# Moving the preparation of the first MLP's output weights eight attention slots later

## The chip, the cores and the metric

The kernel runs on one NeuronCore of a Trainium2 chip, as one program launch. The metric is the device time of that launch in microseconds, the median of several runs. The engines are named as the profile names them: PE is TensorE's matmul side and PEld its weight loads, DVE is VectorE, ACT is ScalarE, POOL is GpSimd and SP is SyncE, whose queue issues the DMAs here.

## The reference: attention with a learned bias, then two MLPs

- Attention over 4 batches, 8 heads, 576 positions, head size 64: `softmax(q k^T / 8 + bias) v`. The bias of head h at row i and column j is a small two-layer net (hidden size 32, ReLU) of `log1p(|i-j|) / log1p(max(i,1))`; it is the same for all batches.
- The result becomes 2304 tokens of 512 numbers.
- First MLP: `h = max(x w1, x w2, x w3)` with 768 columns, then `h w_out`, 768 x 512. These `w_out` weights (`moe_w_out`, `mwo` in the kernel) are the ones the change is about.
- Second MLP: 2048 columns, a quadratic gate, and an output product back to 512.

MLP weights arrive as 64-bit numbers and are turned on the chip into a sum of two float16 parts, hi and lo; products use three matmuls (hi hi, hi lo, lo hi).

## The kernel before: slots, queues and a planner

**Slots.** Attention is cut into 144 slots. A unit is one block j of 128 query rows and one batch b; each of its 8 heads is a slot. Blocks 0, 1 and 2 take slots 0 to 31, 32 to 63 and 64 to 95, 8 per batch; the last 48 slots alternate the short block (64 rows, called SJ, 4 slots per batch) and block 3. In a slot `emit_s` (L691) makes the scores of the next slot on PE, `emit_soft` adds the bias and takes the row's extreme on DVE (L705), takes the exponential on ACT (L707), makes hi and lo (L723 on ACT, L724 and L725 on POOL) and has them transposed by DMA (L727). Three slots later `emit_pv` (L747) multiplies by v.

**Bias.** The bias table of block j+1 is built during block j by 18 `bias_group` calls: a mask on DVE (L389), 16 matmuls (L393), and an eviction on DVE (L399, L400) or on ACT and POOL (L402 to L405) in turn. They need a table of logarithms that a DMA brings (`xtable`, L297, or L302 for the short block) and that is scaled on DVE (L307). Block 2's groups are written for slots 44 to 59.

**First MLP.** When a pair of batches of a block is done, its items go into a queue: 18 `mlp1` groups of 12 matmuls (L802, evicted by L807 on ACT or L809 on DVE, hi and lo by L813 and L814), then 4 `mlp2` groups of 18 matmuls (L824) which need the output weights. Each slot takes items at a fixed rate (2 a slot in block 0, then 1.2, 1.5, ...). Until the output weights are ready, `next_mlp` hands out `mlp1` items of block 0 alone.

**Output weights.** `conv_wo` has 12 pieces and an end. Pieces 1 to 6 each load 128 rows (L450), decode them (L462, L463, L465 on ACT, L464 on DVE), and sum magnitudes on PE for a scale (L481, L483). The decoded numbers stay in a scratch tile, `zt` and `rt_`, parts of `ws`. Pieces 7 to 12 split one stripe each into hi and lo (L157 on ACT, L158 on DVE) in the tile `wo`. Then `wo_done` is set. The parameter `woz` is the first slot that takes decode pieces (0.7 a slot, `c0`), `wo` the first that takes split pieces (1 a slot, `c1`) and from which, once all is done, `next_mlp` hands out everything:

```python
if i >= (WO if n_wo[0] >= NF1 else PRM["woz"]):
    with sooner("wo"):
        for _ in range(rate("conv", PRM["c0"] if n_wo[0] < NF1 else PRM["c1"])):
            if n_wo[0] != NF1 or i >= WO:
                n_wo[0] += 1
                next(pieces, None)
with sooner("mlp"):
    for _ in range(rate("mlp", PRM["mlp"][u.j])):
        e = next_mlp(i >= WO and (wo_done or not PRM["ww"]))
```

The raw buffers for these loads serve the first MLP's input weights until slot 13, and later the second MLP's weights. `rt_` is taken by the short block's `xtable` (L302), which is written for slot 64; its scaling for slot 85.

**Order.** The program text gives priorities (bias groups rank 400 instructions sooner); a planner that simulates the engines lists each engine's instructions, taking what is ready, also from far ahead in the text. The engines then work through their lists in order.

Of the kernel before, what the change touches and what calls it, by code (L numbers as in the profile page):

```python
# [20 lines left out]
def kernel(ctx: ExitStack, tc: tile.TileContext, qt, kt, vr, small, mw1, mw2, mw3, mwo, win, wo2, out):  # L21
# [17 lines left out]
        pin=0,  # L39
        ww=1,  # L40
        vb='pppp',
        woz=28,
        c1=1,
        ef=1,
        vl=[0, 0, 2, 11],
        vm=[0, 0, 8, 15],
        vs=[0, 0, 11, 19],
        wo=38,
        cm=[0, 3, 6, 9, 13, 16],
        veng='vv',  # L50
        weng='vvv',
# [41 lines left out]
    def st(shape, dt, tag):  # L93
        return sb.tile(shape, dt, tag=tag, name=tag, bufs=BUFS.get(tag, 1))
# [3 lines left out]
    wo = st([P, NF1, 512], U32, "wo")  # L98
# [1165 lines left out]
```

## Time and profile before

| what | us |
|---|---|
| median of 3 runs | 1012.7 |
| lowest and highest run | 1000.15, 1017.84 |
| profiled execution, its own time | 1012.1 |
| span of its instructions | 1010.3 |
| PE busy in the span | 927.0 |
| DVE busy | 700.4 |
| ACT busy | 600.4 |
| POOL busy | 511.7 |

Times in a trace are counted from the first instruction, so they add up to the span; the device time of the same execution is 1.8 us more. A view by stretches gives, for each stretch of the span, how long each engine was busy. A timeline gives for each instruction, or a run of equal ones, its start, its length, and in brackets how long its engine had been idle before it and what ended that.

### The profile page before, as it was taken

What the parts mean: (1) busy time and instruction counts of PE and PEld (TensorE: products, weight loads), DVE (VectorE), ACT (ScalarE), POOL (GpSimd) and SP (SyncE); (2) the same over time, 40 slices, a digit from 0 to 9 for tenths busy, and PEclk for the clock granted to TensorE, in tenths of its full rate; (3) what the DMA queues carried; (4) which work ended last, traced back from release to release, by engine and by line L of the source; (5) the groups of instructions that cost most, each with busy time, mean ns of one, the idle gap of its engine ahead of it and who ended that gap; (6) DMA issues with size and microseconds to landing.
All of it is one profiled execution on the core that took longest, in us unless ns stands there. A gap on an engine that the chain in (4) does not pass through costs nothing. (4 is left out here: it accounts for less than half of the span.)

```text
span 1010.3 us, 25953 instructions
## 1 busy us (share of the span) xinstructions
PE 927.0 (92%) x10258; PEld 757.4 (75%) x10258; DVE 700.4 (69%) x1551; ACT 600.4 (59%) x1194; POOL 511.7 (51%) x734
## 2 busy tenths in 40 slices
PE   5758889889999999999999888998999999999996
PEld 5636668678888878778777777543588888888885
DVE  8987877767756686556455487886686587586565
ACT  4788865855656545868577689543354444444342
POOL 4132577666777765646457011997134343344442
PEclk8777979999999999999999999999999999999999
DMA  9896989998998979999999654010020010000000
GB/s 301 247 290 140 245 190 229 207 237 170 207 259 186 187 180 209 215 223 235 209 188 197 184 196 137 22 35 8 1 85 22 1 43 23 1 22 13 10 22 22
DMA packets 238970, 141.47 MB, mean 140 GB/s; under 512 B 187520, under 2 KB 217728, under 8 KB 238336
## 3 DMA queue, kind: packets, MB, share of 16 engines
q1 hardware_dynamic: 238688, 139.55, 58.6%
q8 instruction: 80, 1.31, 0.5%
q14 instruction: 42, 0.34, 0.1%
q10 hardware_dynamic: 160, 0.26, 0.1%
HBM read 79.68 MB, written 15.27 MB: 94 GB/s over the span
## 5 line engine op out<-in xcount | busy, mean ns | idle before, releaser
L802 PEld LDWEIGHTS <-aw 128*128 128x128 f16 x2160 | 190.3, 99 | 46.2 <-issue 24.6
L802 PE MATMUL pm<-xT,aw 128*128 128x256 f16 (+1 forms) x1812 | 202.3, 264 | 7.4 <-ACT hl L829 2.6
L725 POOL TENSOR_TENSOR phl<-sp,phl 128x512 f16<-128x512 f32 x136 | 161.3, 1186 | 0.0
L707 ACT ACTIVATE sp<-sp,mx 128x576 f32<-128x576 f32 x144 | 110.4, 767 | 68.0 <-DVE mx L705 67.7
L691 PE MATMUL s<-k,qz 64*128 64x288 f32 (+1 forms) x576 | 126.2, 449 | 15.4 <-DVE mx L705 13.0
L724 POOL TENSOR_TENSOR phl<-sp,phl 128x64 f16<-128x64 f32 x136 | 49.8, 366 | 178.7 <-ACT phl L723 153.2
L705 DVE CUSTOM_DVE_ANT_0 sp<-s,ab 128x576 f32<-128x576 f32 x128 | 93.3, 752 | 28.4 <-POOL phl L725 10.4
L1142 ACT ACTIVATE sp<-pm,vec 128x256 f32<-128x256 f32 x112 | 61.4, 556 | 81.3 <-PE pm L1125 78.2
L691 PEld LDWEIGHTS s<-k,qz 64*128 64x128 f32 (+1 forms) x576 | 69.1, 195 | 34.6 <-DVE mx L705 15.3
L723 ACT ACTIVATE phl<-sp 128x576 f16<-128x576 f32 x136 | 89.8, 672 | 4.7 <-DMA pt<-phl 3.8
L747 PEld LDWEIGHTS <-pt 128*128 128x128 f16 x1792 | 73.0, 100 | 25.2 <-DMA pt<-phl 16.2
L1146 POOL TENSOR_TENSOR hh<-hh 128x128 f32<-128x128 f32 x56 | 32.9, 588 | 106.4 <-DVE hh L1144 90.3
L747 PE MATMUL pav<-v,pt 128*128 128x64 f16 x1568 | 70.5, 196 | 12.3 <-DMA pt<-phl 11.9
L1125 PEld LDWEIGHTS <-ab 128*128 128x128 f16 x756 | 73.8, 98 | 9.2
L1143 DVE SCALAR_TENSOR_TENSOR hh<-pm,vec,sp 128x256 f32<-128x256 f32 x112 | 52.5, 478 | 33.5 <-ACT sp L1142 33.2
L824 PE MATMUL pm<-hh,wo 128*128 128x256 f16 x558 | 71.3, 279 | 2.6 <-POOL hh L814 1.0
L824 PEld LDWEIGHTS <-wo 128*128 128x128 f16 x648 | 62.2, 100 | 14.7 <-issue 6.5
L814 POOL TENSOR_TENSOR hh<-hm,hh 128x256 f16<-128x256 f32 (+1 forms) x60 | 44.8, 746 | 51.9 <-ACT hh L813 51.7
L1164 PEld LDWEIGHTS <-xT 128*128 128x128 f16 x588 | 57.4, 98 | 7.8 <-ACT xT L1151 1.2
L1164 PEld LDWEIGHTS <-wo 128*128 128x128 f16 x588 | 57.5, 98 | 6.7
L809 DVE SCALAR_TENSOR_TENSOR hm<-pm,hm 128x256 f32<-128x256 f32 (+1 forms) x108 | 42.0, 389 | 28.6 <-PE pm L802 12.3
L1147 POOL TENSOR_TENSOR hh<-hh 128x128 f32<-128x128 f32 x56 | 26.2, 468 | 68.6 <-DVE hh L1144 66.3
(300 smaller groups left out, 1999.0 us busy)
## 6 DMA issues: line engine op xcount, KB each, us to landing
k<-in_k_dram SPq DMA_DIRECT2D x64, 288.0 KB, 3.8
v<-v_d SPq DMA_DIRECT2D x24, 640.0 KB, 4.9
ws<-in_moe_w_out_dram SPq DMA_DIRECT2D x15, 512.0 KB, 4.9
ws<-in_moe_w_in_dram SPq DMA_DIRECT2D x9, 512.0 KB, 6.0
x_d<-hl SPq DMA_DIRECT2D x36, 128.0 KB, 2.5
qz<-in_q_dram SPq DMA_DIRECT2D x16, 256.0 KB, 4.5
ab<-in_moe_w_dram SPq DMA_DIRECT2D x8, 512.0 KB, 9.8
qz<-x_d SPq DMA_DIRECT2D x4, 1024.0 KB, 4.8
```

Source lines behind the costliest of these rows:

```text
L691: last_score[0] = T.matmul(sbox[i + r][:, c, :288], q[p, s if u.j == SJ else s // 2], k[p, 288 * c:288 * c + 288], start=True, stop=True)
L705: last_pair[0] = V.tensor_tensor_reduce(halves(sn), sbox.pop(i)[:, :, :288], halves(bias_sb[u.j][:, h]), -0.125, 3e38, ALU.add, ALU.min, mx)
L707: last_soft[0] = A.activation(pf, sn, AF.Exp, scale=-1.0, bias=mx, accum_out=u.sums[:, h:h + 1])
L723: A.activation(hl[:, :S], pf, AF.Copy)
L725: G.tensor_tensor(hl[:, S + 64:], pf[:, :512], hl[:, :512], ALU.subtract)
L747: T.matmul(u.pav[:, 64 * h:64 * h + 64], pt[:, c], v[:, sl, 64 * (h % 4):64 * (h % 4) + 64], **kw)
L802: T.matmul(o, wm[:, ft, i, wp, kk], x_rhs(key, xp, kk) if n == 256 else x_rhs(key, xp, kk)[:, c], start=(x == 0), stop=(x == 11))
L824: T.matmul(pm, wo16[:, ft, wp, P * d:P * d + P], hh[:, ft, hp], start=(ft == 0 and y == 0), stop=(ft == NF1 - 1 and y == 2))
L1125: T.matmul(pm, w[:, wp, kk], x2t[ORDER[y]][:, kk, xp, 256 * sub:256 * sub + 256], start=(x == 0), stop=(x == 11))
L1142: A.activation(r, pm, AF.Relu, scale=c_ch[:, f], bias=c_half)
L1143: V.scalar_tensor_tensor(t, pm, c_c[:, f], r, ALU.mult, ALU.max)
L1164: T.matmul(m[x], gl[:, gp, i], w[:, wp], start=(start and z == 0 and x % 2 == 0), stop=(stop and z == 2 and (x % 2 == 1 or x == 6)))
```

## The change

Two of the planner's parameters: decode pieces of the first MLP's output weights begin at slot 36, not 28, and their splits, with the output products behind them, from slot 46 on, not 38.

```diff
         pin=0,
         ww=1,
         vb='pppp',
-        woz=28,
+        woz=36,
         c1=1,
         ef=1,
         vl=[0, 0, 2, 11],
         vm=[0, 0, 8, 15],
         vs=[0, 0, 11, 19],
-        wo=38,
+        wo=46,
         cm=[0, 3, 6, 9, 13, 16],
```

## Rows read from the trace of the kernel before

**Rows 1.** The page's head: span, and busy time and instructions by engine.

```profile
span 1010.3 us, 25953 instructions
...
PE 927.0 (92%) x10258; PEld 757.4 (75%) x10258; DVE 700.4 (69%) x1551; ACT 600.4 (59%) x1194; POOL 511.7 (51%) x734
```

**Rows 2.** Busy time by stretches: length, engines' busy time (instructions), clock, DMA, GB/s.

```profile
core 0: us, PE busy (x) PEld busy (x) DVE busy (x) ACT busy (x) POOL busy (x), PEclk, DMA share, GB/s
...
125.00:150.00 25.00, 20.69 (x270) 16.49 (x269) 17.37 (x37) 17.07 (x37) 19.49 (x27) 0.73 0.87 186
150.00:175.00 25.00, 22.55 (x486) 21.02 (x483) 20.80 (x43) 11.14 (x31) 20.06 (x24) 1.00 0.98 246
175.00:200.00 25.00, 20.79 (x245) 15.82 (x243) 19.35 (x65) 21.74 (x49) 15.82 (x23) 1.00 0.96 200
200.00:225.00 25.00, 20.73 (x279) 18.25 (x278) 15.21 (x39) 15.81 (x35) 14.85 (x20) 0.99 1.12 243
225.00:250.00 25.00, 25.00 (x364) 21.01 (x363) 16.06 (x35) 13.16 (x33) 14.42 (x20) 0.94 0.79 163
250.00:275.00 25.00, 24.86 (x357) 21.02 (x355) 18.07 (x39) 16.30 (x41) 20.78 (x25) 1.00 1.06 218
```

**Rows 3.** Timeline of DVE: scores of slots 31, 32, 45, 46, 48.

```profile
147.09 0.76 DVE L705 CUSTOM_DVE_ANT_0 sp<-s,ab 128x576 f32<-128x576 f32 x1
...
174.27 0.76 DVE L705 CUSTOM_DVE_ANT_0 sp<-s,ab 128x576 f32<-128x576 f32 x1 [0.82 <-POOL ab L405]
...
199.21 0.76 DVE L705 CUSTOM_DVE_ANT_0 sp<-s,ab 128x576 f32<-128x576 f32 x1
...
211.07 0.75 DVE L705 CUSTOM_DVE_ANT_0 sp<-s,ab 128x576 f32<-128x576 f32 x1
...
230.27 0.75 DVE L705 CUSTOM_DVE_ANT_0 sp<-s,ab 128x576 f32<-128x576 f32 x1
```

**Rows 4.** Groups by line, 147.8 to 174.2 us: busy us, mean ns, idle before.

```profile
L462 ACT ACTIVATE ws<-ws 128x512 f32<-128x512 f32 x3 | 2.1, 685 | 2.2 <-DMA ws<-in_moe_w_out_dram 2.2
...
L464 DVE SCALAR_TENSOR_TENSOR ws<-ws 128x512 uint32<-128x512 uint32 x1 | 1.1, 1056 | 0.0
```

**Rows 5.** Timeline of ACT: the first decode and the bias eviction behind it.

```profile
151.54 0.68 ACT L462 ACTIVATE ws<-ws 128x512 f32<-128x512 f32 x1 [1.52 <-DMA ws<-in_moe_w_out_dram]
...
154.97 0.37 ACT L402 ACTIVATE btmp<-pm 128x256 f32<-128x256 f32 x1
```

**Rows 6.** Timelines of POOL and DVE: two decodes and a POOL subtraction.

```profile
184.74 1.16 POOL L725 TENSOR_TENSOR phl<-sp,phl 128x512 f16<-128x512 f32 x1
...
184.97 1.47 DVE L464 SCALAR_TENSOR_TENSOR ws<-ws 128x512 uint32<-128x512 uint32 x1 [0.77 <-ACT ws L463]
...
188.28 0.69 DVE L464 SCALAR_TENSOR_TENSOR ws<-ws 128x512 uint32<-128x512 uint32 x1 [0.88 <-ACT ws L463]
```

**Rows 7.** Timelines of ACT, DVE and PE: the six splits and PE's wait.

```profile
204.21 3.78 ACT L157 ACTIVATE wo<-ws,vec 128x512 f16<-128x512 f32 x6
...
204.96 4.81 DVE L158 SCALAR_TENSOR_TENSOR wo<-ws,vec,wo 128x512 f16<-128x512 f32 x6 [1.27 <-ACT wo L157]
...
209.19 1.47 PE L802 MATMUL pm<-xT,aw 128*128 128x256 f16 x12 [0.79 <-ACT hm L807]
```

**Rows 8.** Timelines of DVE and PE: two table scalings, matmuls around the second.

```profile
177.16 0.52 DVE L307 TENSOR_SCALAR xtab<-xtab,vec 128x576 f32<-128x576 f32 x1 [1.25 <-DMA xtab<-log_d]
...
221.89 0.37 DVE L307 TENSOR_SCALAR ws<-ws,vec 128x288 f32<-128x288 f32 x1 [5.68 <-DMA ws<-log_d]
...
217.99 2.13 PE L824 MATMUL pm<-hh,wo 128*128 128x256 f16 x18
...
222.92 0.64 PE L393 MATMUL pm<-coef,masks 128*128 128x64 f16 x16 [2.75 <-DVE masks L389]
...
224.24 3.63 PE L824 MATMUL pm<-hh,wo 128*128 128x256 f16 x18 [0.62 <-DVE ab L400]
```

**Rows 9.** Timelines of POOL and DVE: block 2's last bias group, slot 64.

```profile
271.88 1.05 POOL L405 TENSOR_TENSOR ab<-ab,btmp 128x256 f32<-128x256 f32 x1
...
284.07 0.76 DVE L705 CUSTOM_DVE_ANT_0 sp<-s,ab 128x576 f32<-128x576 f32 x1 [1.26 <-PE s L691]
```

## The prediction, made before the change was run

> **What bounds the kernel now.** I read the page first: TensorE is busy 927.0 of 1010.3 us [rows 1]. The busy time by stretches of 25 us says where the rest could be won. From 225 us on, PE is busy for 25.00 and 24.86 us of 25 [rows 2]; before that it idles 4.31, 2.45, 4.21 and 4.27 us in the four stretches from 125 to 225 us, 15.24 us together. The slots that the change names lie just there. The score instructions of VectorE (L705, one a slot in slot order) date the slots: slot 31 at 147.1 us, slot 32 at 174.3, slot 45 at 199.2, slot 46 at 211.1, slot 48 at 230.3 [rows 3]. So attention stands still for 27.2 us between blocks 0 and 1, while the bias table of block 1 is finished (the row of slot 32 names L405, the end of a bias group, as its releaser), then runs 14 slots in 25 us, then stops again around the splits of the first output weights. In 175 to 200 us ScalarE is the fullest engine, 21.74 of 25 us [rows 2].
>
> **What moves, by the code.** Decode pieces come at 0.7 a slot, splits at one a slot. Working the rates through, the six decodes are written at slots 29, 30, 32, 33, 35, 36 before and 37, 38, 40, 41, 43, 44 after; the six splits at 38 to 43 before and 46 to 51 after; the first output product (L824) is allowed at slot 44 before and 52 after. The 18 groups of mlp1 for token pair (0,1) may run either way (order below 2): at 1.2 a slot from slot 37 they are used up at slot 51, so no MLP turn is lost. From slot 55 on both versions write the same instructions in the same order. Nothing is added or removed; the change can only move PE's idle time between 147 us and about 260 us, and through the planner what follows. PE is full behind it, so I price each step by the PE idle it makes or removes. A gain through this window alone is at most the 15.24 us above.
>
> **Part by part**, against the profiled execution's own 1012.1 us (0.6 us under the median of the runs, 1012.7):
>
> 1. Decode 0 leaves the standstill of 147 to 174 us. There stand three L462 (685 ns each) and one L464 of 1056 ns [rows 4]. L464 sits on VectorE, which builds the bias: 1.1 us. ScalarE also waits for the raw weights before 151.54 us, and the next L402 (a bias group's eviction) follows only at 154.97 us [rows 5], but VectorE has other groups meanwhile. Ends: 0, and -2.45, all of PE's idle time in 150 to 175 us [rows 2]. I take -1.1, VectorE's row being the nearest.
>
> 2. The same work arrives at slots 37 to 41, where ScalarE is fullest: three L462 and the two other ScalarE instructions of decode 0, allowed the same length, 5 x 0.685 = 3.4 us. ScalarE's idle time there is 25 - 21.74 = 3.3 us [rows 2], scattered between waits. Ends 0 and +3.4; in between no row decides, and I take half, +1.7. VectorE's share is hidden by its 5.65 idle us there.
>
> 3. The six splits leave 204 to 210 us: 3.78 us of ScalarE and 4.81 us of VectorE in one block [rows 7]. PE lost 0.79 us to it, waiting for an eviction (L807) behind the block. Ends -0.8 and 0; I take -0.8.
>
> 4. They arrive at slots 46 to 51, one a slot, beside bias groups of block 2. Cover: VectorE is busy 15.21 and 16.06 us of 25 in the stretches from 200 to 250 us, and PE has mlp1 of (0,1) to fill with. Taken 0; without that cover +4.8, the VectorE block at its length.
>
> 5. The table load of the short block (L302) reuses the decode's scratch, so it waits for the last split; its scaling (L307) then stops VectorE until it lands: 5.68 us idle before 221.89 us. PE loses 2.75 us to it and comes back slow: 18 matmuls of L824 take 3.63 us where 18 took 2.13 just before [rows 8], and the granted clock of 225 to 250 us is 0.94 [rows 2], so 1.5 us more. After the change this falls later, beside a longer PE queue. Ends: -4.25 (another table's scaling waited 1.25 us only [rows 8]) and +2.9 (PE sees all 5.68). I take -1.5: the wait stays, the slow clock goes.
>
> 6. The DMAs move with it: six raw loads, two table loads, four result stores of the first output products and the first loads for the second MLP, all on SP's queue among the transposes. Their bytes are the same and the raw buffers are free long before, so 0; the raw loads' own waits on ScalarE (2.2 us of the standstill, [rows 4]) are in step 1's bounds.
>
> Sum: -1.1 + 1.7 - 0.8 + 0 - 1.5 = -1.7, so 1012.1 - 1.7 = 1010.4, **1010 us**. All low ends together: -2.45 - 0.8 - 4.25 = -7.5, 1005; all high ends: 3.4 + 4.8 + 2.9 = +11.1, 1023.
>
> **A port rule to weigh.** L464 takes 0.69 us at 188.28 us and 1.47 us at 184.97 us, where POOL is in a subtraction that began at 184.74 us and lasts 1.16 [rows 6]. A split has the same kind of operands, so at its new place, among POOL's bias and hi/lo work, I allow it 0.78 us more. The Trainium skill, SBUF — State Buffer, section "Who interferes with whom", says that VectorE and GpSimd share a read port that is locked for a whole instruction: a VectorE instruction with two SBUF inputs and a GpSimd one that reads SBUF exclude each other. The pair of rows agrees with it. By that rule all six splits are stretched, and the sum would be up to 6 x 0.78 = 4.7 us higher, an estimate of 1015 us, if nothing hides it; I keep it at 0 as in step 4, and its full length in rival A.
>
> **Rivals.**
>
> A, slower: VectorE cannot finish block 2's bias in time. It gets the splits stretched, 4.81 + 6 x 0.78 = 9.5 us, and the 5.68 us wait of step 5, 15.2 us, into the slots in which that bias is made. Its last group now ends at 271.88 + 1.05 = 272.9 us, and slot 64, which needs it, starts at 284.07 [rows 9]: 11.1 us of slack. Past that attention stands still as at 147 us; 15.2 - 11.1 = 4.1 us late, all idle on PE if nothing fills: 1016 us. For it: VectorE is the bias's engine and was late once already [rows 3]. Against: the first standstill cost PE only 2.45 us.
>
> B, faster by more: ScalarE free of the decode and its wait lets the L402 of 154.97 us go when the wait began, at 151.54 - 1.52 = 150.0 us, 5 us sooner; block 1 starts as much earlier, and the idle time of 150 to 175 us and of 200 to 225 us goes with the slow clock: 2.45 + 4.27 + 1.5 = 8.2, 1004 us. For it: ScalarE is busy 11.14 of 25 us there, mostly waiting. Against: VectorE is at 20.80 [rows 2].
>
> C, it does nothing: the planner takes whatever is ready. L302, written for slot 64, and L307, written for slot 85, run before slot 48 [rows 3, 8]; decodes whose data are in may be pulled back to the same idle places. 1012 us.
>
> D, the whole list is planned anew and a later stretch comes out otherwise. No row prices that; one more standstill like the 27 us one with PE unfed, or one less, is about 22 us either way: 990 or 1034.
>
> **How the numbers follow.** Forecast 0.46, A 0.14, B 0.14, C 0.12, D 0.07 on each side. The runs of the kernel before spread from 1000.15 to 1017.84 us, so the median to come can be some us off its trace; the range takes the bounds 1005 to 1023 and B, and a few us of spread beyond both: 997 to 1026. Two per cent (992 and 1033 us) is about what a measurement can tell from no change. Only D reaches it, and the tail of A: faster 0.07, same 0.85, slower 0.08.
>
> **What would show it.** Step 1: the gap between slots 31 and 32 shorter than 27.2 us by one or two. Step 2: ScalarE over 22 us busy in the 25 us after slot 32, with all six L464 there or later. Steps 3 and 4: splits one at a time, beside L389, and the first L824 after all of mlp1 (0,1). Step 5: L302 later than slot 48 and the wait of L307 without a fall of the granted clock. A: slot 64's score released by L405. C: L464 and the splits at the old times. The prediction is wrong if PE's idle time after 225 us changes by more than that before it.

## The result, and the profile after

| kernel | median, us | lowest to highest | runs |
|---|---|---|---|
| before | 1010.58 | 1000.15 to 1020.1 | 20 |
| after | 1017.36 | 1011.06 to 1023.17 | 20 |

The change makes the kernel slower: ratio 1.0074, 95% interval 1.0056 to 1.0093, so about 7.5 us with 1.9 us either way. Single executions of one kernel spread by up to about 1% to each side; the profiled one of after took 1016.85 us, its span 1015.1. Ratios, here and below, leave out single runs more than 1.5% above the fastest of their kernel, so they are not quite the quotient of the medians.

The page after, busy time of the engines (answers [rows 1]):

```profile
PE 922.4 (91%) x10258; PEld 754.4 (74%) x10258; DVE 702.7 (69%) x1551; ACT 599.8 (59%) x1194; POOL 515.1 (51%) x734
```

The instructions are the same in number on every engine. The first five stretches of [rows 2], with the same columns:

```profile
125.00:150.00 25.00, 21.77 (x288) 17.96 (x288) 16.95 (x37) 15.13 (x34) 18.88 (x27) 0.71 0.96 198
150.00:175.00 25.00, 19.33 (x401) 18.07 (x401) 18.12 (x36) 12.18 (x33) 17.21 (x21) 0.93 0.92 218
175.00:200.00 25.00, 23.22 (x322) 19.62 (x322) 16.18 (x49) 17.30 (x42) 15.43 (x23) 1.00 0.90 163
200.00:225.00 25.00, 18.63 (x270) 14.69 (x271) 18.34 (x56) 18.73 (x41) 16.83 (x21) 1.00 1.15 261
225.00:250.00 25.00, 23.53 (x311) 19.29 (x310) 20.18 (x39) 15.42 (x38) 19.49 (x24) 0.94 1.05 224
```

In 150 to 175 us PE idles 5.67 us (25 - 19.33) where it idled 2.45. Fixed stretches cut the work at another place in each kernel, so the rest is read by slots: the score instruction (L705) of a slot starts a stretch. Busy time by such stretches, kernel before, slots 31 to 32, 32 to 46, 46 to 64 and 120 to 143:

```profile
147.09:174.27 27.18, 24.73 (x552) 23.20 (x550) 22.38 (x44) 13.46 (x36) 22.62 (x28) 1.00 0.96 237
174.27:211.07 36.80, 31.80 (x370) 25.42 (x368) 28.19 (x85) 30.81 (x67) 22.83 (x33) 1.00 0.99 223
211.07:284.07 73.00, 69.38 (x985) 58.71 (x983) 46.02 (x105) 41.65 (x103) 50.45 (x65) 0.98 0.99 202
...
479.31:549.31 70.00, 65.44 (x834) 52.30 (x833) 34.30 (x89) 48.69 (x107) 39.66 (x56) 0.98 0.96 189
```

The same four of after:

```profile
144.94:176.70 31.76, 24.91 (x531) 23.43 (x528) 21.90 (x43) 14.93 (x38) 23.39 (x28) 0.95 0.92 204
176.70:215.70 39.00, 34.52 (x467) 28.16 (x464) 23.64 (x73) 28.77 (x66) 23.07 (x33) 1.00 1.02 210
215.70:285.30 69.60, 64.50 (x907) 54.38 (x908) 52.48 (x120) 44.27 (x107) 51.80 (x65) 0.98 0.96 208
...
480.39:552.93 72.54, 65.15 (x834) 52.30 (x833) 35.27 (x89) 48.68 (x107) 39.66 (x56) 0.98 0.94 183
```

From slot 31 to 64 TensorE does the same work but for two matmuls, 1907 before (552 + 370 + 985) and 1905 after, in 136.98 and 140.36 us. The standstill between slots 31 and 32 is 4.6 us longer, not shorter. From slot 64 on, each engine has the same instructions in the same order in both kernels; yet slots 120 to 143 take 2.5 us more in this trace.

What VectorE waited for in the standstill, kernel before (columns: what waited, for what; us in total, times, longest):

```profile
DVE btmp L399 <- PE pm L393: 2.0, 2, 1.7
DVE masks L389 <- PE pm L393: 1.4, 2, 0.8
DVE sp L705 <- POOL ab L405: 0.8, 1, 0.8
```

and after:

```profile
DVE ws L464 <- ACT ws L463: 2.7, 2, 1.4
DVE rd L756 <- ACT sp L707: 2.7, 1, 2.7
...
```

Two waits are new. One is for the decode (L463 to L464); one is for ScalarE's exponential (L707), at the first step of a finished unit's normalization (L756). The timelines of after show where both come from. ScalarE (start, us, instruction, idle before and its releaser): a wait for a hi/lo buffer with the exponential of slot 31 behind it, the raw-load waits and the block of splits:

```profile
147.74 0.68 ACT L723 ACTIVATE phl<-sp 128x576 f16<-128x576 f32 x1 [2.44 <-DMA pt<-phl]
148.33 0.76 ACT L707 ACTIVATE sp<-sp,mx 128x576 f32<-128x576 f32 x1
...
154.38 0.68 ACT L462 ACTIVATE ws<-ws 128x512 f32<-128x512 f32 x1 [1.42 <-DMA ws<-in_moe_w_out_dram]
...
157.50 0.66 ACT L462 ACTIVATE ws<-ws 128x512 f32<-128x512 f32 x1 [1.87 <-DMA ws<-in_moe_w_out_dram]
...
197.68 0.68 ACT L462 ACTIVATE ws<-ws 128x512 f32<-128x512 f32 x1 [2.12 <-DMA ws<-in_moe_w_out_dram]
...
205.99 0.68 ACT L463 ACTIVATE ws<-ws 128x512 uint32<-128x512 uint32 x1 [2.23 <-DMA ws<-in_moe_w_out_dram]
...
221.65 3.79 ACT L157 ACTIVATE wo<-ws,vec 128x512 f16<-128x512 f32 x6 [1.49 <-DVE vec L514]
```

VectorE of after: scores of slots 31 and 32 (as in [rows 3]; 45 is at 211.54, 46 at 215.70, 48 at 222.28), two decodes and one eviction of `mlp1` (L809) behind a late decode:

```profile
144.94 0.76 DVE L705 CUSTOM_DVE_ANT_0 sp<-s,ab 128x576 f32<-128x576 f32 x1
...
155.66 1.18 DVE L464 SCALAR_TENSOR_TENSOR ws<-ws 128x512 uint32<-128x512 uint32 x1 [1.33 <-ACT ws L463]
...
158.74 0.69 DVE L464 SCALAR_TENSOR_TENSOR ws<-ws 128x512 uint32<-128x512 uint32 x1 [1.37 <-ACT ws L463]
...
176.70 0.76 DVE L705 CUSTOM_DVE_ANT_0 sp<-s,ab 128x576 f32<-128x576 f32 x1
...
209.93 0.42 DVE L809 SCALAR_TENSOR_TENSOR hm<-pm,hm 128x256 f32<-128x256 f32 x1 [4.50 <-ACT hm L807]
```

TensorE of after, the matmuls that waited for those two engines, and the ones behind the splits:

```profile
157.09 0.63 PE L393 MATMUL pm<-coef,masks 128*128 128x64 f16 x16 [1.33 <-DVE hm L809]
159.44 1.00 PE L802 MATMUL pm<-xT,aw 128*128 128x128 f16 x12 [1.72 <-ACT hm L807]
...
209.95 0.93 PE L802 MATMUL pm<-xT,aw 128*128 128x256 f16 x7 [1.86 <-ACT hm L807]
...
223.39 0.49 PE L747 MATMUL pav<-v,pt 128*128 128x64 f16 x11 [3.50 <-DMA pt<-phl]
...
224.51 4.12 PE L802 MATMUL pm<-xT,aw 128*128 128x256 f16 x21
```

The first chain is to be read across the three: a raw row lands late, ScalarE waits 1.42 us at L462, VectorE waits 1.33 us at L464 for ScalarE's L463, with the eviction L809 queued behind it, and PE waits 1.33 us for L809. 3 us later it happens again: 1.87 us on ScalarE, 1.37 on VectorE, and PE waits 1.72 us for an eviction (L807) that ScalarE has queued behind the row. At 206 us it happens once more. The wait at L756 is not a raw row's, the first of which is asked for only at 148.6 us: ScalarE stands 2.44 us at L723, until 147.74 us, for a hi/lo buffer that a transposition still reads, and the exponential that L756 needs is queued behind. How long ScalarE waited for raw rows in all, kernel before (us, times):

```profile
  ACT ws L462: 3.7, 4
```

and after:

```profile
  ACT ws L462: 6.0, 4
  ACT ws L463: 2.2, 1
```

### The profile page after: what moved, and what is told of

It is laid out like the page before. It is cut to its first block, busy times and chain, and to the rows that moved or that the text cites. A ratio compares the mean times of both kernels' runs of the same rounds, so it can differ in the third digit from the quotient of the medians.

```text
span 1015.1 us, 25955 instructions
## 1 busy us (share of the span) xinstructions
PE 922.4 (91%) x10258; PEld 754.4 (74%) x10258; DVE 702.7 (69%) x1551; ACT 599.8 (59%) x1194; POOL 515.1 (51%) x734
## 5 line engine op out<-in xcount | busy, mean ns | idle before, releaser
L725 POOL TENSOR_TENSOR phl<-sp,phl 128x512 f16<-128x512 f32 x136 | 160.0, 1176 | 0.0
L707 ACT ACTIVATE sp<-sp,mx 128x576 f32<-128x576 f32 x144 | 110.6, 768 | 71.9 <-DVE mx L705 71.3
L691 PE MATMUL s<-k,qz 64*128 64x288 f32 (+1 forms) x576 | 121.3, 449 | 11.3 <-DVE mx L705 8.9
L705 DVE CUSTOM_DVE_ANT_0 sp<-s,ab 128x576 f32<-128x576 f32 x128 | 93.0, 751 | 31.0 <-PE s L691 13.4
L747 PEld LDWEIGHTS <-pt 128*128 128x128 f16 x1792 | 71.9, 100 | 30.1 <-DMA pt<-phl 21.4
L723 ACT ACTIVATE phl<-sp 128x576 f16<-128x576 f32 x136 | 89.9, 672 | 4.4 <-DMA pt<-phl 3.7
L1146 POOL TENSOR_TENSOR hh<-hh 128x128 f32<-128x128 f32 x56 | 35.6, 635 | 109.0 <-DVE hh L1144 94.3
L691 PEld LDWEIGHTS s<-k,qz 64*128 64x128 f32 (+1 forms) x576 | 66.5, 196 | 28.9 <-DVE mx L705 10.9
L1143 DVE SCALAR_TENSOR_TENSOR hh<-pm,vec,sp 128x256 f32<-128x256 f32 x112 | 52.5, 478 | 36.0 <-ACT sp L1142 35.9
L824 PE MATMUL pm<-hh,wo 128*128 128x256 f16 x558 | 68.5, 273 | 1.9 <-ACT hh L813 1.1
L824 PEld LDWEIGHTS <-wo 128*128 128x128 f16 x648 | 61.2, 98 | 11.8 <-issue 4.0
L809 DVE SCALAR_TENSOR_TENSOR hm<-pm,hm 128x256 f32<-128x256 f32 (+1 forms) x108 | 42.0, 390 | 35.0 <-ACT hm L807 17.9
L1147 POOL TENSOR_TENSOR hh<-hh 128x128 f32<-128x128 f32 x56 | 26.2, 468 | 63.8 <-DVE hh L1144 61.6
```

What stands on the lines that cost most here:

```text
L691: last_score[0] = T.matmul(sbox[i + r][:, c, :288], q[p, s if u.j == SJ else s // 2], k[p, 288 * c:288 * c + 288], start=True, stop=True)
L705: last_pair[0] = V.tensor_tensor_reduce(halves(sn), sbox.pop(i)[:, :, :288], halves(bias_sb[u.j][:, h]), -0.125, 3e38, ALU.add, ALU.min, mx)
L707: last_soft[0] = A.activation(pf, sn, AF.Exp, scale=-1.0, bias=mx, accum_out=u.sums[:, h:h + 1])
L723: A.activation(hl[:, :S], pf, AF.Copy)
L725: G.tensor_tensor(hl[:, S + 64:], pf[:, :512], hl[:, :512], ALU.subtract)
L747: T.matmul(u.pav[:, 64 * h:64 * h + 64], pt[:, c], v[:, sl, 64 * (h % 4):64 * (h % 4) + 64], **kw)
```

## The experiments

Ratios are to the runs of the kernel before that were made beside them. The kernel before had medians of 1011.36, 1011.82, 1013.28 and 1011.8 us in the four sets. One trace moves by several us where nothing differs (slots 0 to 16, same order in all, take 55.5 to 62.1 us), so stretches are compared over several traces where there are several.

### Only the decodes late

```
-        woz=28,
+        woz=36,
```

> Decodes from slot 36 as in the change, but the splits' bound left at slot 38, so they follow the last decode and the output products come at slot 51. Theory D (the late decodes cost the time, because they run among block 1's first 14 slots, where ScalarE is full): slower than before by 5 to 9 us, like the change, ratio 1.005 to 1.009. Rival F (the later output products cost it, through what fills PE): much the same, since they come late here too, 1.004 to 1.009. Rival S (the bound of the splits costs it): within 2 us of before.

1016.43 us, ratio 1.0048 (1.0017 to 1.0080). The decodes' bound alone makes the kernel slower, by an amount whose interval holds the change's. Its standstill is 31.3 us, like the change's. Each engine has the change's order of instructions here up to 242 us, so this run does not separate theory D from rival F.

### Only the splits late

```
-        wo=38,
+        wo=46,
```

> Decodes from slot 28 as before, bound of splits and output products at slot 46. Theory D: within 2 us of before, ratio 0.998 to 1.002. Rival F: slower by 5 to 9 us, 1.005 to 1.009. Rival S: the same 5 to 9 us.

1013.0 us, ratio 0.9967 (0.9929 to 1.0005). The splits stay where they were: the slot is only a lower bound on where they are written, and the planner draws them forward while their decodes are early. The first output product (L824) does come late here, at slot 53 as against 47 before and 54 in the change, and costs nothing: rival F falls, and rival S with it. The loss hangs on the decodes.

### The change, with the decodes held behind the last soft step

```
-                    with sooner("wo"):
+                    with sooner("wo"), tc.issue_after(last_soft[0].ins):
```

> The change, and every piece of the output weights is issued only after its own slot's exponential, so no decode can be planned into the standstill between slots 31 and 32. Theory D: as slow as the change or slower, 1.006 to 1.012, with the decodes at slots 37 to 45 and the standstill at 27 us or less. Rival H (the two decodes that the planner drew into the standstill made it longer, 31.8 against 27.2 us, and that is the cost): back to the kernel before or better, 0.996 to 1.002.

1021.34 us, ratio 1.0089 (1.0059 to 1.0120). Now no decode runs before slot 37; the edit holds the splits too, which come one by one from 227 to 243 us. Slots 31 to 32 and 32 to 46 of this kernel:

```profile
147.60:176.78 29.18, 23.36 (x526) 21.69 (x524) 21.06 (x42) 10.66 (x30) 23.16 (x27) 1.00 0.83 184
176.78:218.68 41.90, 40.01 (x455) 30.60 (x453) 25.28 (x74) 32.94 (x72) 21.66 (x32) 0.92 1.00 208
```

The standstill is 2.6 us shorter than in after but still 2 us longer than before; in the next stretch PE is busy 40 us for 455 matmuls, at a granted clock of 0.92. Theory D's ratio came (1.006 to 1.012), its standstill of 27 us or less did not, and rival H's ratio did not either. But holding the pieces costs time of its own, 116.3 us for slots 32 to 64 (a mean of 108.1 before, table below), so this run can't say what the two decodes in the standstill cost. What VectorE waited for in this standstill:

```profile
...
DVE rd L756 <- ACT sp L707: 2.5, 1, 2.5
```

No L464 is among its waits; the exponential's wait has stayed, behind a wait of 2.06 us at L723, although no decode runs in this standstill.

### The two kernels again, unchanged

No edit: the change once more with timing, and single traces of the kernel before (twice) and of the change, to have several traces of each.

> The changed kernel, unaltered, for a second trace and a second comparison. Theory D: 1.005 to 1.009; slot 64 later than in the kernel before by at least 3 us, most of it by slot 46. If only noise separated the two traces: slot 64 anywhere within 3 us of before, ratio still 1.005 to 1.009, and the delay found later, in stretches that have the same order of instructions.

> The kernel before, unaltered, for another trace. All five traces so far have one order of instructions from slot 64 on, yet in the change and its repeat a result store keeps ScalarE waiting before slot 126 (2.6 us) and a raw load before the end of attention (1.1 to 2 us). Theory P (the change's delay leads to these waits each time): neither is in this trace; slot 120 to 143 takes 70 us, slot 143 to the end 461 us. Theory L (luck of the transfers): they turn up here as often as in the change, 72 to 73 us and 462 us in about half the traces.

> As the run before it, a further trace of the kernel before. In both theories the part from slot 16 to slot 64 takes 192 us, the standstill in it 27 us.

> The changed kernel, unaltered, a third trace. Theory P: slot 120 to 143 in 72 to 73 us, slot 143 to the end in 462 us or more. Theory L: either value. In both the standstill takes 31 us, slots 32 to 46 39 us, slots 46 to 64 70 us, slot 16 to 64 193 us.

The change repeats: 1020.15 us, ratio 1.0072 (1.0044 to 1.0101). The single executions were 1008.6 and 1008.82 (before) and 1013.26 us (after). Two kernels with a third buffer (below) have the same order of instructions up to slot 96 as the kernel before and the change; with their traces there are four of each, and a mean of each stretch can be had (us from score to score):

| slots | before (4 traces) | mean | change (4 traces) | mean | difference |
|---|---|---|---|---|---|
| 16 to 31 | 55.0, 53.1, 49.3, 52.6 | 52.5 | 52.6, 51.5, 51.8, 50.9 | 51.7 | -0.8 |
| 31 to 32 | 27.2, 27.0, 27.8, 26.5 | 27.1 | 31.8, 31.1, 31.7, 29.9 | 31.1 | +4.0 |
| 32 to 46 | 36.8, 36.3, 36.5, 37.1 | 36.7 | 39.0, 39.6, 38.1, 38.4 | 38.8 | +2.1 |
| 46 to 64 | 73.0, 69.3, 70.9, 72.2 | 71.4 | 69.6, 71.5, 70.8, 70.5 | 70.6 | -0.8 |
| 64 to 96 | 116.0 in all | 116.0 | 116.0 in all | 116.0 | 0 |

So +4.5 us of the 7.5 lies between slots 16 and 64, and the standstill, whose four values don't overlap, carries most of it. Those of slots 32 to 46 don't overlap either, but there the change has 97 matmuls more (467 against 370) and behind them 78 fewer; slots 32 to 64 together take 105.7 to 109.8 us before and 108.6 to 111.1 in the change, which overlap. The delay has to be counted from slot 31: slot 64 of the change's second trace starts at 284.5 us, 0.4 later than in the first trace of the kernel before and not by the 3 us or more that theory D had, since its slots before 31 ran faster. In the four standstills of the change VectorE waits 2.7, 3.0, 3.6 and 1.7 us at L464 and 2.7, 1.8, 1.8 and 1.5 us at L756; in those of before 0, 0.7, 0.4, 0.4 and 0, 0, 1.7, 0. The means differ by 2.4 and 1.5 us, 3.9 together, against the 4.0 by which the standstill is longer. That is an account by waits, and the second part of it, which the kernel before has in one trace of four, is not the raw rows'.

### The mirror image: eight slots earlier

```
-        woz=28,
+        woz=20,
...
-        wo=38,
+        wo=30,
```

> Decodes from slot 20 and splits from slot 30, as much earlier than the kernel before as the change is later. Theory D (late decodes lie in the way of block 1's first slots): the stretch from slot 32 to 46 under 36 us, since at most one decode is left in it, but three in the standstill, which grows to 28 to 30 us; in all within 4 us of before or faster, ratio 0.994 to 1.003. Rival T (any shift from the tuned place costs, whichever way): slower by 5 us or more.

In it the splits overwrite values of batch 3 that the last products of block 0 still read, so part of the output differs; the instructions are the same in kind and number. 1022.8 us, ratio 1.0115 (1.0077 to 1.0154). Slots 64 to 96 of it, which take 116.0 to 116.2 us everywhere else:

```profile
282.03:407.05 125.02, 120.91 (x1619) 99.89 (x1617) 81.71 (x201) 66.32 (x163) 79.17 (x108) 1.00 0.88 185
```

Theory D missed: slots 32 to 46 take 49.2 us, not under 36, and the time is rival T's. Earlier is no gain either, but it loses at another place, with another order of everything up to some 670 us: it says nothing of the change's mechanism.

### The change, with the raw rows fetched early

```
+        wo_load = lambda ft: raw_load(mwo[P * ft:P * ft + P, :], raws[:, ft % 2])
...
-                raw_load(mwo[P * ft:P * ft + P, :], raws[:, ft % 2])
...
+                ft + 2 < NF1 and wo_load(ft + 2)
...
+                with sooner("att"):
+                    if i == 22:
+                        for ft in (0, 1):
+                            wo_load(ft)
```

The line taken out stood at the head of a decode; the one with `ft + 2` stands at its end, so that a row is fetched two decodes ahead. The last four lines take the place of a branch that no parameter set here uses.

> The change, but the raw rows for the first two decodes are loaded at slot 22 and each later one right behind the decode two before it. The planner then puts decodes 0 and 1 at slots 26 and 28, the other four stay at 39, 39, 41, 45 as in the change, the splits at 49. Theory S (the loss is decodes 0 and 1, which wait for their raw rows inside the standstill between slots 31 and 32): back at the kernel before, ratio 0.997 to 1.003, standstill 27 us with PE idle 3 us in it, not 31 and 7. Rival M (the loss is the four decodes among slots 39 to 45, where ScalarE is full): as the change, 1.004 to 1.009, with slots 32 to 46 still 39 us.

1016.92 us, ratio 1.0039 (1.0007 to 1.0072): by the estimate about half of the loss is gone, though the interval reaches from almost none of it to nearly all. It lies between what S and M had. With their rows in, decodes 0 and 1 run ahead of the standstill. Slots 31 to 32, 32 to 46 and 46 to 64 of this kernel:

```profile
146.02:173.46 27.44, 23.22 (x493) 20.99 (x491) 21.19 (x43) 11.72 (x33) 22.40 (x28) 1.00 0.90 209
173.46:211.60 38.14, 34.35 (x467) 28.15 (x464) 23.64 (x72) 28.75 (x66) 23.05 (x33) 1.00 1.03 215
211.60:280.84 69.24, 62.84 (x907) 53.52 (x908) 51.65 (x119) 44.43 (x107) 52.16 (x65) 1.00 0.99 210
```

The standstill is back at 27.4 us, and slots 31 to 64 take 134.8 us against a mean of 135.2 before. From about 168 us on each engine has the change's order again, with its late decodes, its block of splits and its late output products, and slots 32 to 64 take 107.4 us (107.9 with a third buffer besides, below), where the kernel before takes 108.1 in the mean: what the change has behind the standstill costs nothing there, against rival M's reason. What VectorE waited for in this standstill:

```profile
...
DVE rd L756 <- ACT sp L707: 0.3, 1, 0.3
```

No L464 is among them, and the exponentials' wait is 0.3 us: both new waits are gone. ScalarE still waits 6.2 us for raw rows in all (8.1 in the kernel below that has a third buffer besides, with a standstill of 27.4 us too), so the length of those waits in all does not decide. The edit does two things at once, it brings the rows early and takes the two decodes out of the standstill; no run here tells which of the two counts.

### The kernel before, with the raw rows fetched early

The same edit on the kernel before.

> The kernel before with the same early loads: decodes at slots 26, 28, 36, 37, 39, 43 instead of 28, 31, 36, 37, 37, 41. Theory S: no decode is left in the standstill, so 0 to 3 us faster than before, 0.996 to 1.001. Rival M: the later decodes come two slots later, so 1 to 3 us slower, 1.000 to 1.004.

1018.26 us, ratio 1.0052 (1.0019 to 1.0086): slower, where theory S had no change or a gain. No L464 runs in its standstill, and yet that takes 29.4 us. Slots 32 to 46 and 46 to 64:

```profile
175.84:209.17 33.33, 26.96 (x289) 19.46 (x287) 20.13 (x68) 25.68 (x58) 20.68 (x30) 0.80 0.99 202
209.17:292.82 83.65, 79.74 (x1087) 67.73 (x1085) 52.89 (x123) 47.55 (x114) 53.25 (x68) 0.98 0.92 197
```

The first has 81 matmuls fewer than before, the second 102 more, and PE runs at a granted clock of 0.80 in the first; the two together take 117.0 us against 108.1 before. Early raw rows are no gain by themselves. ScalarE waits 3.4 us for raw rows here, no less than the 3.3 us of the kernel before (mean of four traces), so the run does not say whether fewer such waits would help.

### Half the way

```
-        woz=28,
+        woz=32,
...
-        wo=38,
+        wo=42,
```

> Decodes from slot 32 and splits from 42, half the change: the planner puts decodes 0 and 1 in the standstill as in the change, the others at slots 37, 37, 40, 41 nearly as before, splits at 43. Theory S: as slow as the change, 1.004 to 1.009, standstill 31 us. Rival M: as before, 0.998 to 1.003.

1020.95 us, ratio 1.0078 (1.0042 to 1.0115): the whole loss at half the shift. Decodes 0 and 1 run in the standstill here too (30.6 us), so S has the ratio and the length. But its reason is not there. Of VectorE's waits in this standstill:

```profile
DVE rd L756 <- ACT sp L707: 2.6, 1, 2.6
...
DVE ws L464 <- ACT ws L463: 0.5, 1, 0.5
```

ScalarE waits 3.7 us for raw rows in all, as in the kernel before, and VectorE 0.5 us at L464. So late rows do not lengthen this standstill; what it has in common with the change is decode 0 in the standstill and the wait at L756 (behind 2.52 us at L723). The loss doesn't grow with the distance of the shift.

### A third buffer for the results of the output products

What was open: slots 120 to 143 took 71.9 to 72.8 us in three traces of the change and 70.0 to 70.4 in three of before, with the same order of instructions. (Theory P had 461 us behind slot 143 in the kernel before and 462 or more in the change; 461.9 and 460.1 against 461.0 do not bear it out.) In after ScalarE waits there for a result's store to land before it may write the next:

```profile
504.91 0.62 ACT L829 ACTIVATE hl<-pm,vec 128x128 f32<-128x128 f32 x2 [7.49 <-DMA x_d<-hl]
```

At the same instruction it is idle for 5.49 and 4.91 us in the other two traces of the change, and for 4.91, 4.87 and 4.29 in those of the kernel before, where TensorE's product came last in the first and the store in the other two. So the kernel before waits for this store too, only less long. Three kernels, the one before, the change, and the change with early rows, each got this edit:

```
+        n_hl = [0]
...
-            t = st([P, 256], F32, "hl")
+            n_hl[0] += 1
+            t = thr.bitcast(F32)[:, :256] if n_hl[0] > 16 and n_hl[0] % 3 == 0 else st([P, 256], F32, "hl")
```

> The kernel before, and from the seventeenth output product on every third result (L829) is written into the thresholds' tile, which nothing reads any more by then, in place of one of the two buffers of hl: three buffers instead of two, so ScalarE need not wait for a result's store to land before it writes the next. Theory W (after slot 96 the change loses because ScalarE waits for a store of the first output products, with every later ScalarE instruction behind it): in the kernel before this wait is not what ends last there (4.91 us idle, ended by TensorE), so 0.999 to 1.001, slots 120 to 143 in 70 us. Theory V (the later loss is the chance phase of transfers and clock, no one wait): the same, 1.000, or a shift either way of up to 2 us.

> The change with the same third buffer. W: slots 120 to 143 take 70 to 70.5 us instead of 71.9 to 72.8, ScalarE's 7.5 us wait for the store at L829 is gone, and the ratio to the kernel before falls from 1.0072 to about 1.005. V: the wait goes but TensorE waits for the next thing; slots 120 to 143 stay at 72 us or more and the ratio at 1.007.

> The change with the early raw loads and the third buffer together. W, with the raw loads' lateness as the cause of the loss before slot 64: the window as in the run with early loads alone (slot 31 to 64 in about 135 us) and slots 120 to 143 in 70 to 71 us, so 1.0039 less 0.002 to 0.004: 1.000 to 1.002, the loss all but gone. V: 1.004 as with the early loads alone.

| kernel | ratio without | ratio with the third buffer | interval |
|---|---|---|---|
| before | 1 | 0.9975 | 0.9941 to 1.001 |
| change | 1.0072 | 1.0042 | 1.001 to 1.0074 |
| change, early rows | 1.0039 | 1.0010 | 0.9979 to 1.004 |

Medians: 1010.55, 1014.75 and 1012.56 us. Slots 120 to 143 in the kernel before with it:

```profile
476.70:543.64 66.94, 64.64 (x843) 52.18 (x842) 34.38 (x89) 48.83 (x107) 40.87 (x57) 1.00 1.05 201
```

and in the change with it:

```profile
485.24:551.94 66.70, 63.63 (x834) 51.45 (x833) 34.38 (x89) 48.86 (x107) 39.70 (x56) 1.00 1.04 198
```

The only wait for a store in this stretch of the change with the third buffer is 0.50 us, at 509.42 us. The stretch is 67 us in both, 3 us less than before and 5 to 6 less than in the change, and 68.3 us in the change with early rows. So the wait for the store is real, and theory V, which left the stretch at 72 us or more, falls. But the ratio falls by 0.0025 to 0.0030 in all three kernels, the one before included: as far as intervals of 0.003 each way tell, it is a cost of both kernels, not of the change alone. Theory W holds for the stretch and is not borne out for the time: the change with the third buffer stands to the kernel before with it as 1.0042 to 0.9975, 1.0067, near what it was, though intervals of this width leave room for a gain of 0.002 as well. The early rows, on the other hand, give 0.0033 to 0.0032 back in both comparisons (1.0072 to 1.0039, 1.0042 to 1.0010), though in each of them the two intervals overlap. No version is shown to beat the kernel before: the best, 0.9975, has 1 in its interval.

**What stays open.** Of the loss of 0.0072 the early rows take back 0.0033. The other 0.0035 to 0.0039 (1.0039 without, and 1.0010 against 0.9975 with the third buffer) do not lie between slots 31 and 64, which take 134.8 and 135.2 us in the two traces with early rows, and were not placed. In the first of these two, slots 120 to 143 take 74.4 us, the longest of all traces; but they take 69.7 us in the kernel with held decodes and in the kernel before with early rows, which are both slower than the kernel before, so their length does not follow the loss. Open is also what makes the standstill longer in general. In the change, VectorE's waits at L464 and L756 add up to it; the half shift has nearly as much with 0.5 us at L464, and the kernel before with early rows has 2 us of it with no wait at either.

## Why the prediction was wrong

The forecast was -1.7 us and the result about +7.5. The time lies in the range, and within 2%, but on the other side of no change; that it is near the 1016 of rival A is luck, since A's mechanism did not occur.

**Step 1** (decode 0 leaves the standstill, -1.1, ends 0 and -2.45) failed, in its premise. Decode 0 was not in the standstill of before: its L464 ran at 135.96 us, ahead of slot 31; the L464 of [rows 4] and the L462 of [rows 5] are decode 1's, and two of the three L462 are the first steps of 2 and 3. The change put decodes 0 **and** 1 there, because the planner draws a decode that is written for a later slot (37 and 38) forward into an idle place. The standstill grew by 4.0 us in the mean of four traces, in place of shrinking by 1.1. I counted where pieces are written and took that for where they run, although [rows 4] showed three L462 to one L464, the parts of several decodes and not one whole.

**Step 6** (DMAs 0) failed with it. The bytes are the same, but where the kernel before issued its first raw load at 124.1 us, the change issues it at 148.6 us, within the standstill, and ScalarE waits for raw rows 8.2, 5.8, 8.2 and 5.7 us in the four traces of the change, 3.7, 4.6, 1.4 and 3.4 before. I said that the buffers are free long before; they are, but a load isn't issued earlier for that, as it stands at the head of its own decode. The row of [rows 5], 1.52 us of ScalarE before a decode, was the price per late row; behind it stood VectorE's L464, which I had as 1.1 us of work and not as a place where VectorE stops: 2.4 of the 4.0 us, by the waits. For the wait at L756, the other 1.5, I had no term at all.

**Step 2** (the work arrives at slots 37 to 41, +1.7) failed with step 1: decode 0 ran in the standstill, and slots 32 to 46 hold four L464, those of decodes 2 to 5, in both kernels, with ScalarE busy for 28.77 us against 30.81. That slots 32 to 46 grew by 2.1 us, near my number, is luck: they hold 97 matmuls more, and the next slots 78 fewer. I had also counted three L462 to a decode, which has one. What I named as a sign of it, ScalarE over 22 us busy in the stretch after slot 32, was not seen: it is busy 17.30 us in 175 to 200, and waits for raw rows at 197.68 and 205.99 us.

**Step 3** (splits leave 204 to 210 us) came true, and **step 4** (one a slot) did not: the planner ran them as a block again, six L157 from 221.65 us, and PE stood 3.50 us before 223.39 us, waiting for a transposed tile, and came back slow, 21 matmuls in 4.12 us; whether the splits made that tile late is not shown. **Step 5** was right that L302 comes later than slot 48 (230.79 us against slot 48 at 222.28) and that the wait shrinks:

```profile
235.62 1.13 DVE L307 TENSOR_SCALAR ws<-ws,vec 128x288 f32<-128x288 f32 x1 [2.14 <-DMA ws<-log_d]
```

2.14 us in place of 5.68 [rows 8]. But the granted clock of 225 to 250 us is 0.94 again, now behind PE's 3.50 us without work. I had -2.3 for steps 3 to 5; slots 46 to 64 gave -0.8 in the mean, with 78 matmuls fewer and values that overlap, so the sum of these steps is not shown either way.

**What the sum left out.** I took PE for full behind 225 us, from two stretches of 25 us. In slots 120 to 143 it is idle for 4.6 us of 70 in the kernel before already, so time could be lost there too; the 0.0035 to 0.0039 of the loss that the early rows don't give back had no term, and no run places it.

**The port rule.** The decodes of after agree with it once more: L464 takes 1.53 us at 195.02 us, where POOL's L725 began at 194.85 us, and 0.69 at 202.41. For the splits it cost little. VectorE's share of the first two and of the last two, at the new place (the third and fourth take 1.40 us):

```profile
223.63 1.41 DVE L158 SCALAR_TENSOR_TENSOR wo<-ws,vec,wo 128x512 f16<-128x512 f32 x2
...
227.22 2.02 DVE L158 SCALAR_TENSOR_TENSOR wo<-ws,vec,wo 128x512 f16<-128x512 f32 x2
```

and POOL beside them:

```profile
226.54 1.02 POOL L404 TENSOR_TENSOR btmp<-btmp,xtab 128x256 f32<-128x256 f32 x1 [3.15 <-ACT btmp L402]
227.63 1.06 POOL L405 TENSOR_TENSOR ab<-ab,btmp 128x256 f32<-128x256 f32 x1
```

Four splits take 0.70 us each, the first three of them while POOL waits for ScalarE; the last two run beside POOL at 1.01. Together 4.83 us, against 4.81 in [rows 7]. What the Trainium skill, SBUF — State Buffer, section "Who interferes with whom", says of the two engines fits both; the trace decides the sum: none of the 4.7 us.

**The rivals.** A (block 2's bias late, 1016): its last group ends at 274.2 us (273.47 + 0.72) and slot 64 starts at 285.30, released by a score matmul; the slack is as before [rows 9]. B did not occur. C (the planner hoists, 1012) had the mechanism half right: decodes were drawn back to idle places, but not to the old ones, and not harmlessly. I had the planner as a reason for no change; it was what moved the two decodes into the standstill. D (the list behind planned anew) did not occur: the order from slot 64 on is the same. The test that I had set, that PE's idle time after 225 us must change less than that before it, came out against me too: in the two traces it rose from 15.2 to 17.1 us between 125 and 225 us, and by more, from 4.6 to 7.4 us, in slots 120 to 143 alone, a stretch that the third buffer makes equal in both kernels, without a closed difference in time being shown.

## What to carry to other kernels

Where a planner or scheduler may draw work forward, a slot in the source is a bound and not a place: count in the trace which pieces run in the idle stretch now, by their number, before pricing what leaves it. A step that starts with its own load can stop more than its own engine where the row isn't in: here a row late by 1.42 us on ScalarE stopped VectorE and PE for 1.33 us each, through what was queued behind. Price the queue behind the wait, and then the whole order that comes out: the same early loads took the growth out of the change's standstill and made the kernel before slower. And when a change loses under 1%, several traces of both kernels are needed before a stretch may be blamed: here one stretch of identical order differed by 2.5 us, and making it equal was not shown to close the difference.

## What the runs showed of the hardware that was not expected

Six raw rows of the same size took 4.1 to 7.2 us from issue to landing before and 4.2 to 8.4 us after (medians 4.5 and 5.5). A result store of 128x256 values landed in 1.7 to 6.7 us in after; with two buffers ScalarE was idle for 4.3 to 7.5 us before a result that waited for one (five traces of the two kernels), with three the one wait in those slots of the change was 0.5 us. The same instructions in the same order took 55.5 to 62.1 us (slots 0 to 16) in one trace and another, while slots 64 to 96, where PE is busy for 114 of 116 us, took 116.0 to 116.2 us in every kernel that kept their order.
